# A long convolution and two MLP blocks in one kernel: the inverse transform in column tiles of TensorE, the filter's second weights in row tiles, and one merged product

## The chip, the cores and the metric

The kernel runs on one core of one Trainium2 chip. The metric is the device time of one execution in microseconds (us), given as the median of several runs; one more execution was profiled.

## The reference

```python
def _attn_ref(x, v, pos_emb, w1, w2):              # x, v: 1 x 12480 x 128
    h_mlp = np.maximum(pos_emb @ w1, 0.0) @ w2     # w1: 64 x 64, w2: 64 x 128
    h_filt = h_mlp * np.exp(-0.01 * np.arange(S))[:, None]
    u = x * v
    Uf = np.fft.rfft(u, n=2 * S, axis=1)
    Hf = np.fft.rfft(h_filt, n=2 * S, axis=0)
    y = np.fft.irfft(Uf * Hf[None, :, :], n=2 * S, axis=1)[:, :S, :]
    return x * y

def _moe_ref(x, w_in, w_out):                      # 128 -> 2048 -> 128
    r = np.maximum(x @ w_in, 0.0)
    return (r * r) @ w_out

def _moe2_ref(x, w_in, w_out):
    h = x @ w_in
    return (h / (1.0 + np.exp(-1.702 * h))) @ w_out
# output: _moe2_ref(_moe_ref(_attn_ref(...)))
```

All inputs are 32-bit floats here, except that the MLP weights arrive as 64-bit floats and are split on the chip.

## The kernel before

The long convolution is a transform of length 99 x 127 in two steps (N1 = 99, N2 = 127), with 64 folded columns (NJ). It runs in stages, all in an order written out by hand; each engine works its own queue in that order.

The filter stage (`filter_stage`, line 245) makes the hidden features of the filter. The first transform (`s1_step`, line 266) works the features and then the product of x and v: each step takes four channels, and for each channel two halves, whose 64 outputs go to partitions 0 to 63 and 64 to 127 of one PSUM tile; the two halves stand in turn in PE's order. ScalarE (ACT) copies the result to G or A (line 267). G goes through DRAM (`gd`) on SP's queue.

The frequency stage is `stage_s2`. It runs over 50 pairs p of the 99 frequencies. For each pair `spectra` multiplies the transposed features with w2b (`hk`, line 316) and the data with the coefficients (`xk`, line 318), two matmuls of 256 columns each; `back` goes back with the product P (`ob`, line 342), and every second pair `features` does four frequencies' features (`fk`, line 305, 128 columns each) for the pairs to come. A frequency's features stand in f_t as 128 rows, 64 for the cosine part and 64 for the sine part. w2b is a block matrix, 128 x 256: w2 stands in the upper left block for the cosine part, and again in the lower right one for the sine part; the rest is zero. ACT copies hk to hc (line 320), fk to fs (line 308) and ob to bs (line 346), and its queue stores bs to DRAM (`bd`) and loads `Gs`. VectorE (DVE) multiplies xk with hc in two products (line 329) and takes the difference (line 334); GpSimd (POOL) takes the sum (line 333). `load_m` (line 276) asks on SP's queue for the coefficients (m) of the pair five further on, into seven buffers; it stands behind `back(p - 2)`, which frees a buffer. `work.tick` (class `Weights`) puts one step of each running weight conversion on DVE and ACT behind each pair, and asks for raw weights on SP's queue; two chunks are left for the stage's end.

The MLP stage (`mlp`) runs over 25 tiles of about 500 positions. Each MLP has 8 units a tile, and the second one is 40 units behind the first; PE does 12 matmul records for a unit's inputs (`hin`) and outputs (`acc`, four units later), lines 488 to 490. The last step of the inverse (`inverse`, line 446) makes a tile's y in PSUM (`yps`): five segments of 98 or 99 columns, each with two accumulating fp32 matmuls over 99 rows. `front_y` calls it for tile t + 1 among the units of tile t. Two segments that are left over (`REST`) are done once, by `front_rest`. Each fp32 matmul leaves two weight loads and two matmul records in the trace; those of the MLP, in the faster 32-bit format fp32r, leave one of each.

At the seam of the two stages `load_b` reads the inverse's rows back from `bd`, DVE and POOL combine them (`combine`, line 393), and `spare` matmuls stand on PE before and behind tile 0's inverse.

Of the kernel before, what the change touches and what calls it, by code (L numbers as in the profile page):

```python
# [9 lines left out]
FP32 = mybir.dt.float32  # L10
# [4 lines left out]
ALU = mybir.AluOpType  # L15
# [8 lines left out]
N1, N2 = 99, 127  # L24
# [3 lines left out]
D = 128  # L28
F = 64
# [3 lines left out]
NP = -(-N1 // 2)  # L33
# [5 lines left out]
FK = 4  # L39
# [52 lines left out]
def conv_mlp_kernel(ctx: ExitStack, tc: tile.TileContext, xc, xt, vc, pt, w1, w2,  # L92
                    moe_w_in, moe_w_out, moe2_w_in, moe2_w_out,
                    c_s1, c_s2, c_i2, c_win, out):
    nc = tc.nc
# [5 lines left out]
    ci2 = const.tile([N1, 2, N1], FP32, name="ci2")  # L101
# [169 lines left out]
    def load_m(mp, p):  # L271
        if p >= NP:
            return
        n = min(2, N1 - 2 * p)
        m_t[p] = mp.tile([128, 2, 2, 128], FP32, tag="m", name="m", bufs=7)
        nc.sync.dma_start(out=m_t[p][:, 0:n], in_=c_s2[:, 2 * p:2 * p + n])

    def load_h(mp, g, queue=nc.scalar):
        if g >= NHL:
            return  # L280
        n = min(HL, N1 - g * HL)
        h_t[g] = mp.tile([128, HL, 2 * F], FP32, tag="Gs", name="Gs", bufs=2)
        queue.dma_start(out=h_t[g][:, 0:n], in_=gd[:, g * HL:g * HL + n])

    def stage_s2(sp, mp, A, w2b, hooks, work):


        kp = tc.tile_pool(name="kp", bufs=2, space=PSUM, reuse_waits="tile")
        obp = tc.tile_pool(name="obp", bufs=2, space=PSUM, reuse_waits="tile")
        P_t, k_t, bs_t, f_t = {}, {}, {}, {}  # L290

        def pair(p):
            return min(2, N1 - 2 * p)

        with kp as kp, obp as obp:
            def features(g):


                if g >= NFK:
                    return  # L300
                n = min(FK, N1 - g * FK)
                ps = kp.tile([128, FK, 128], FP32, tag="fk", name="fk", bufs=1)
                for i in range(n):
                    k = g * FK + i
                    nc.tensor.matmul(out=ps[:, i], lhsT=h_t[k // HL][:, k % HL, :],  # L305
                                     rhs=m_t[k // 2][:, k % 2, 0, :])
                f_t[g] = sp.tile([128, FK, 128], FP32, tag="fs", name="fs", bufs=2)
                nc.scalar.copy(out=f_t[g][:, 0:n], in_=ps[:, 0:n])

            def spectra(p):  # L310
                n, m = pair(p), m_t[p]
                xk = kp.tile([128, 2, 2, D], FP32, tag="xk", name="xk", bufs=3)
                hk = kp.tile([128, 2, 2, D], FP32, tag="hk", name="hk", bufs=2)
                for j in range(n):
                    k = 2 * p + j
                    nc.tensor.matmul(out=hk[:, j], lhsT=f_t[k // FK][:, k % FK, :], rhs=w2b)  # L316
                for j in range(n):
                    nc.tensor.matmul(out=xk[:, j], lhsT=m[:, j, 0, :], rhs=A[:, 2 * p + j])  # L318
                hc = sp.tile([128, 2, 2, D], FP32, tag="hc", name="hc", bufs=2)
                nc.scalar.copy(out=hc[:, 0:n], in_=hk[:, 0:n])  # L320
                k_t[p] = xk, hc

            def product(p):
                n = pair(p)
                xk, hc = k_t.pop(p)
                t = []
                for c in range(2):
                    t.append(sp.tile([128, 2, 2, D], FP32, tag=f"t{c}", name=f"t{c}", bufs=2))
                    nc.vector.tensor_tensor(  # L329
                        out=t[c][:, 0:n], in0=xk[:, 0:n, c].unsqueeze(2).to_broadcast([128, n, 2, D]),  # L330
                        in1=hc[:, 0:n], op=ALU.mult)
                P = sp.tile([128, 2, 2, D], FP32, tag="P", name="P", bufs=3)
                nc.gpsimd.tensor_tensor(out=P[:, 0:n, 1], in0=t[0][:, 0:n, 1], in1=t[1][:, 0:n, 0], op=ALU.add)  # L333
                nc.vector.tensor_tensor(out=P[:, 0:n, 0], in0=t[0][:, 0:n, 0], in1=t[1][:, 0:n, 1],
                                        op=ALU.subtract)
                P_t[p] = P

            def back(p):
                n, m, P = pair(p), m_t.pop(p), P_t.pop(p)
                ob = obp.tile([128, 2, 2, D], FP32, tag="ob", name="ob")  # L340
                for j in range(n):
                    nc.tensor.matmul(out=ob[:, j], lhsT=m[:, j, 1, :], rhs=P[:, j])  # L342
                g, o = divmod(2 * p, HK)
                if o == 0:
                    bs_t[g] = sp.tile([128, HK, 2, D], FP32, tag="bs", name="bs", bufs=2)
                nc.scalar.copy(out=bs_t[g][:, o:o + n], in_=ob[:, 0:n])
                if o + n == HK or p == NP - 1:
                    nc.scalar.dma_start(
                        out=bd[:, :, HK * g:HK * g + o + n].rearrange("h j k c d -> (h j) k c d"),
                        in_=bs_t.pop(g)[:, 0:o + n])  # L350

            features(0)
            for p in range(NP + 2):
                if p < NP:
                    spectra(p)
                if p % 2 == 0:
                    features(p // 2 + 1)
                if 0 <= p - 2:
                    back(p - 2)
                load_m(mp, p + 5)  # L360
                if p % 4 == 1:
                    load_h(mp, p // 4 + 2)
                if 0 <= p - 1 < NP:
                    product(p - 1)
                work.tick(p)
                for f in hooks.get(p, ()):
                    f()
            work.finish()
# [4 lines left out]
    def tile_parts(segs):  # L373

        at = 0
        for j, s, r, n in segs:
            yield j, s, r, n, at
            at += n
# [34 lines left out]
    def mlp(lp, cp):  # L413
# [26 lines left out]
        def inverse(ps, segs):  # L440


            for j, s, r, w, o in tile_parts(segs):
                b = b_t[j // JG][1][:, j % JG, 0 if s > 0 else 1]
                for c in range(2):
                    nc.tensor.matmul(out=ps[:, o:o + w], lhsT=b[:, c, :], rhs=ci2[:, c, r:r + w],  # L446
                                     start=(c == 0), stop=(c == 1))

        def front_y(t):

# [123 lines left out]
        for n in range(len(seq) + LAG):  # L574
# [3 lines left out]
            if n < len(seq):  # L578
                l, t, j = seq[n]
# [24 lines left out]
    with tc.manual_schedule():  # L604
# [13 lines left out]
        def advance():  # L618
            if steps[0] in folds:
                inputs.fold()  # L620
            inputs.load()
            steps[0] += 1

        with tc.tile_pool(name="h", bufs=1) as hp:
            h = hp.tile([N1, F, 2 * NJ], FP32, name="h")
            inputs = Inputs(up)
# [10 lines left out]
        with tc.tile_pool(name="A", bufs=1, reuse_waits="tile") as ap_, ExitStack() as mps:  # L637
            A = ap_.tile([128, N1, 2, D], FP32, name="A")
            for d in range(0, D, 4):
                s1_step(bank, inputs.u[d // XC], d % XC, A[:, :, :, d:d + 4])  # L640
                if d // 4 in (0, 3, 6, 9):
                    q = 25 * (d // 12)
                    q = slice(q, min(q + 25, N1))
                    nc.sync.dma_start(out=gd[:, q], in_=G[:, q].rearrange("p k c f -> p k (c f)"))
                if d // 4 < 22:
                    advance()
                if d // 4 == 22:
                    assert inputs.done == NXC
                    vps.close()
                    mp = mps.enter_context(tc.tile_pool(name="mh", bufs=1, reuse_waits="tile"))  # L650
                    w2b = mp.tile([128, 2 * D], FP32, name="w2b")
                    nc.sync.dma_start(out=w2b, in_=w2)
                if 22 <= d // 4 < 27:
                    load_m(mp, d // 4 - 22)
                if d // 4 in (23, 25):
                    load_h(mp, (d // 4 - 23) // 2, nc.sync)
            sgs.close()
            ups.close()
            w0 = ctx.enter_context(tc.tile_pool(name="w0", bufs=1, side="right", reuse_waits="tile"))
            split_weights(w0, 0)  # L660
            cp = ctx.enter_context(tc.tile_pool(name="cvt", bufs=1, side="right", reuse_waits="tile"))
            lp = ctx.enter_context(tc.tile_pool(name="lp", bufs=2, side="right", reuse_waits="tile"))
            nc.sync.dma_start(out=ci2, in_=c_i2)
            work = Weights([0, 4, 1, 5, 2, 6], 3, 7, 5, cp, [(44, 3), (46, 7)])
            hooks = {44: [lambda: load_x(lp, 0)]}
            with tc.tile_pool(name="s2", bufs=1, side="right", reuse_waits="tile") as sp:
                stage_s2(sp, mp, A, w2b, hooks, work)
# [92 lines left out]
```

## Time and profile before

| | |
|---|---|
| median of 3 runs | 1419.97 us (1417.61 to 1421.13) |
| profiled execution | 1419.01 us, of it 1417.2 us span |
| TensorE (PE) busy | 1399.3 us, 99% |
| VectorE (DVE) busy | 1114.3 us, 79% |
| ScalarE (ACT) busy | 940.4 us, 66% |
| frequency stage | about 90 to 242 us |
| MLP stage | from about 253 us |

Times in the rows are microseconds from the start of the span unless they are marked ns. PE is TensorE's matmuls, PEld its weight loads, which overlap with them. A matmul's recorded duration holds its way through the array, so records that follow each other overlap; what one costs is read from start to start, or from the chain. In the chain, each piece is the time that it alone added.

### The profile page before, as it was taken

How to read it: one execution, taken by the hardware profiler on the slowest of the kernel's cores; microseconds unless marked ns; L12 is line 12 of the kernel's file. 1: busy time of each engine (PE TensorE's matmuls, PEld its weight loads, DVE VectorE, ACT ScalarE, POOL GpSimd, SP SyncE). 2: the span in 40 equal slices, each digit the busy share in tenths (PEclk: the TensorE clock that was granted, in tenths of full speed). 3: DMA queues.
4: the chain of work that ended last, by engine and by line, in shares of the span. 5: the costliest groups of instructions: out<-in, count | busy, mean ns of one | idle time of the engine just before them, and what ended most of it. 6: DMA issues, size and time to landing. Idle time of an engine off the chain costs nothing.

```text
span 1417.2 us, 17764 instructions
## 1 busy us (share of the span) xinstructions
PE 1399.3 (99%) x7018; PEld 1175.7 (83%) x7018; DVE 1114.3 (79%) x1233; ACT 940.4 (66%) x1066; POOL 221.2 (16%) x209
## 2 busy tenths in 40 slices
PE   7999999999999999999999999999999999999998
PEld 7888888788788888888888888888888888888887
DVE  7558988699887777777778777777778787777887
ACT  1654544577667767776767767777777767777776
POOL 3012222425620111111100211012101120000000
PEclk9999999899999999999999999999999999999999
DMA  9977765312200001000010000010000100000000
GB/s 248 302 247 241 242 229 195 102 60 79 68 20 8 26 20 38 25 9 20 27 38 8 27 20 26 8 38 19 27 27 8 38 19 8 8 8 1 15 15 15
DMA packets 46400, 91.34 MB, mean 64 GB/s; under 512 B 4183, under 2 KB 30604, under 8 KB 45804
## 3 DMA queue, kind: packets, MB, share of 16 engines
q1 hardware_dynamic: 36750, 64.71, 15.2%
q10 hardware_dynamic: 9566, 25.49, 4.7%
q8 instruction: 55, 0.90, 0.3%
q14 instruction: 29, 0.24, 0.1%
HBM read 64.33 MB, written 25.85 MB: 64 GB/s over the span
## 4 chain that ended last, share of the span: by engine, by line
PE 92%; DVE 4%; issue 1%; DMA 1%; ACT 1%; POOL 0%; SPq 0%; DVEq 0%; POOLq 0%; ACTq 0%
PE hin L489 12%; PE hin L490 12%; PE hin L488 12%; PE acc L489 12%; PE acc L488 12%; PE acc L490 12%; PE s L266 5%; PE yps L446 4%; PE hk L316 3%; PE xk L318 3%; PE ob L342 3%; PE fk L305 2%; DVE gl L526 1%; DVE r L250 1%; DMA uv<-bd 1%
## 5 line engine op out<-in xcount | busy, mean ns | idle before, releaser
L526 DVE TENSOR_TENSOR gl<-g,gh 128x1004 fp32r<-128x1004 f32 (+4 forms) x400 | 491.7, 1229 | 34.9 <-ACT gh L522 34.5
L506 ACT ACTIVATE g<-hin 128x1004 f32<-128x1004 f32 (+4 forms) x200 | 201.2, 1006 | 238.4 <-PE hin L490 237.9
L488 PE MATMUL acc<-gh,w 128*128 128x502 f32 (+4 forms) x800 | 313.6, 392 | 0.3 <-DVE lo L435 0.3
L488 PE MATMUL hin<-hi,w 128*128 128x502 f32 (+4 forms) x800 | 312.8, 391 | 0.0
L489 PE MATMUL acc<-gl,w 128*128 128x502 f32 (+4 forms) x800 | 311.8, 390 | 0.8 <-DVE gl L526 0.8
L489 PE MATMUL hin<-lo,w 128*128 128x502 f32 (+4 forms) x800 | 312.5, 391 | 0.0
L490 PE MATMUL hin<-hi,w 128*128 128x502 f32 (+4 forms) x800 | 311.9, 390 | 0.0
L490 PE MATMUL acc<-gh,w 128*128 128x502 f32 (+4 forms) x800 | 311.7, 390 | 0.0
L517 DVE TENSOR_TENSOR g<-hin,g 128x1004 f32<-128x1004 f32 (+4 forms) x200 | 238.7, 1193 | 50.6 <-ACT g L509 50.5
L393 POOL TENSOR_TENSOR b<-uv 99x256 f32<-99x256 f32 x127 | 158.1, 1274 | 698.4 <-DMA uv<-bd 501.0
L515 DVE CAST gh<-g 128x1004 fp32r<-128x1004 f32 (+4 forms) x200 | 142.4, 712 | 149.7 <-ACT g L507 149.6
L509 ACT ACTIVATE g<-hin 128x1004 f32<-128x1004 f32 (+4 forms) x200 | 200.1, 1001 | 75.2 <-PE hin L490 67.2
L507 ACT ACTIVATE g<-g 128x1004 f32<-128x1004 f32 (+4 forms) x200 | 208.0, 1040 | 6.4
L522 ACT CAST gh<-g 128x1004 fp32r<-128x1004 f32 (+4 forms) x200 | 202.8, 1014 | 0.4 <-DVE g L517 0.4
L488 PEld LDWEIGHTS hin<-hi,w 128*128 128x128 f32 x800 | 151.4, 189 | 33.8 <-ACT g L506 2.5
L489 PEld LDWEIGHTS acc<-gl,w 128*128 128x128 f32 x800 | 151.1, 189 | 32.0 <-DVE gl L526 2.1
L490 PEld LDWEIGHTS hin<-hi,w 128*128 128x128 f32 x800 | 151.4, 189 | 30.7
L488 PEld LDWEIGHTS acc<-gh,w 128*128 128x128 f32 x800 | 151.2, 189 | 30.8 <-DVE lo L435 0.7
L489 PEld LDWEIGHTS hin<-lo,w 128*128 128x128 f32 x800 | 151.3, 189 | 30.6 <-issue 0.5
L490 PEld LDWEIGHTS acc<-gh,w 128*128 128x128 f32 x800 | 150.8, 189 | 30.4
L329 DVE TENSOR_TENSOR t<-xk,hc 128x512 f32<-128x512 f32 (+1 forms) x100 | 63.8, 679 | 23.7 <-PE xk L318 19.5
L333 POOL TENSOR_TENSOR P<-t,t 128x256 f32<-128x256 f32 (+1 forms) x50 | 43.8, 876 | 176.8 <-DVE t L329 94.5
(56 smaller groups left out, 1032.1 us busy)
## 6 DMA issues: line engine op xcount, KB each, us to landing
uv<-bd SPq DMA_DIRECT2D x64, 198.0 KB
m<-in_c_s_dram SPq DMA_DIRECT2D x49, 256.0 KB
bd<-bs ACTq DMA_DIRECT2D x24, 512.0 KB
x<-in_xc_dram SPq DMA_DIRECT2D x16, 384.0 KB
v<-in_vc_dram SPq DMA_DIRECT2D x16, 384.0 KB
Gs<-gd ACTq DMA_DIRECT2D x10, 512.0 KB
gd<-G SPq DMA_DIRECT2D x3, 1600.0 KB
raw<-in_moe_w_in_dram SPq DMA_DIRECT2D x8, 512.0 KB
```

Of the source, the lines that this page charges most:

```text
L266: nc.tensor.matmul(out=ps[j, e], lhsT=src[:, d + e, j], rhs=cs1[:, half])
L393: engine.tensor_tensor(out=b[:, :, s, c], in0=uv[:, 0, :, c], in1=uv[:, 1, :, 1 - c], op=ALU.add if s != c else ALU.subtract)
L488: nc.tensor.matmul(out=out, lhsT=a, rhs=hl[0], start=first, stop=False)
L489: nc.tensor.matmul(out=out, lhsT=a, rhs=hl[1], start=False, stop=False)
L490: nc.tensor.matmul(out=out, lhsT=b, rhs=hl[0], start=False, stop=last)
L506: nc.scalar.activation(out=g, in_=ps, func=ACTF.Relu)
L507: nc.scalar.activation(out=g, in_=g, func=ACTF.Square)
L509: nc.scalar.activation(out=g, in_=ps, func=ACTF.Sigmoid, scale=1.702)
L515: nc.vector.tensor_copy(out=gh, in_=g)
L517: nc.vector.tensor_tensor(out=g, in0=ps, in1=g, op=ALU.mult)
L522: nc.scalar.copy(out=gh, in_=g)
L526: nc.vector.tensor_tensor(out=gl, in0=g, in1=gh.bitcast(FP32), op=ALU.subtract)
```

## The change

The change has three parts.

In `inverse`, each matmul of 128 weight columns becomes two of 64 weight columns, for output partitions 0 to 63 and 64 to 127, with the same moving columns.

In the frequency stage, w2b becomes 128 x 128: w2 twice, one above the other. The matmuls for hk leave `spectra` for a new function `filters`, which works four frequencies at once, every second pair, ahead of `spectra`. For each frequency it issues two matmuls, one on the 64 rows of the cosine part and one on the 64 rows of the sine part, into two banks of PSUM. ACT copies the four frequencies' result to hc in one instruction, which also brings the two parts of a frequency next to each other. hk has one buffer of two banks instead of two buffers of one bank.

In `product`, the two products become one of 1024 elements, with both operands broadcast, into one tile t. P has two buffers instead of three.

```diff
-                hk = kp.tile([128, 2, 2, D], FP32, tag="hk", name="hk", bufs=2)
-                for j in range(n):
-                    k = 2 * p + j
-                    nc.tensor.matmul(out=hk[:, j], lhsT=f_t[k // FK][:, k % FK, :], rhs=w2b)
...
-                hc = sp.tile([128, 2, 2, D], FP32, tag="hc", name="hc", bufs=2)
-                nc.scalar.copy(out=hc[:, 0:n], in_=hk[:, 0:n])
-                k_t[p] = xk, hc
+                k_t[p] = xk
...
+            def filters(g):
+                n = min(FK, N1 - g * FK)
+                hk = kp.tile([128, 2, FK, D], FP32, tag="hk", name="hk", bufs=1)
+                for i in range(n):
+                    for c in range(2):
+                        f = slice(c * F, (c + 1) * F)
+                        nc.tensor.matmul(out=hk[:, c, i], lhsT=f_t[g][f, i, :], rhs=w2b[f])
+                h_c[g] = sp.tile([128, FK, 2, D], FP32, tag="hc", name="hc", bufs=2)
+                nc.scalar.copy(out=h_c[g][:, 0:n], in_=hk[:, :, 0:n].rearrange("p c k d -> p k c d"))
...
             def product(p):
                 n = pair(p)
-                xk, hc = k_t.pop(p)
-                t = []
-                for c in range(2):
-                    t.append(sp.tile([128, 2, 2, D], FP32, tag=f"t{c}", name=f"t{c}", bufs=2))
-                    nc.vector.tensor_tensor(
-                        out=t[c][:, 0:n], in0=xk[:, 0:n, c].unsqueeze(2).to_broadcast([128, n, 2, D]),
-                        in1=hc[:, 0:n], op=ALU.mult)
-                P = sp.tile([128, 2, 2, D], FP32, tag="P", name="P", bufs=3)
...
+                xk, o = k_t.pop(p), 2 * p % FK
+                hc = h_c[2 * p // FK][:, o:o + n]
+                t = sp.tile([128, 2, 2, 2, D], FP32, tag="t", name="t", bufs=2)
+                full = [128, n, 2, 2, D]
+                nc.vector.tensor_tensor(out=t[:, 0:n], in0=xk[:, 0:n].unsqueeze(3).to_broadcast(full),
+                                        in1=hc.unsqueeze(2).to_broadcast(full), op=ALU.mult)
+                P = sp.tile([128, 2, 2, D], FP32, tag="P", name="P", bufs=2)
...
             for p in range(NP + 2):
+                if p < NP and p % 2 == 0:
+                    filters(p // 2)
                 if p < NP:
                     spectra(p)
...
                 for c in range(2):
-                    nc.tensor.matmul(out=ps[:, o:o + w], lhsT=b[:, c, :], rhs=ci2[:, c, r:r + w],
-                                     start=(c == 0), stop=(c == 1))
+                    for d in (slice(0, D // 2), slice(D // 2, D)):
+                        nc.tensor.matmul(out=ps[d, o:o + w], lhsT=b[:, c, d], rhs=ci2[:, c, r:r + w],
+                                         start=(c == 0), stop=(c == 1))
...
-                    w2b = mp.tile([128, 2 * D], FP32, name="w2b")
+                    w2b = mp.tile([128, D], FP32, name="w2b")
...
+    laid['w2'] = np.concatenate([inputs['w2']] * 2)
```

## Rows read from the trace of the kernel before

**Rows 1.** The page's busy times by engine and the chain that ended last.
```profile
PE 1399.3 (99%) x7018; PEld 1175.7 (83%) x7018; DVE 1114.3 (79%) x1233; ACT 940.4 (66%) x1066; POOL 221.2 (16%) x209
...
PE 92%; DVE 4%; issue 1%; DMA 1%; ACT 1%; POOL 0%; SPq 0%; DVEq 0%; POOLq 0%; ACTq 0%
```

**Rows 2.** Windows of the two stages: stretch, length, then each engine's busy us.
```profile
92.36:238.80 146.44, 145.28 (x764) 130.30 (x765) 126.63 (x192) 71.79 (x124) 41.76 (x48) 1.00 0.68 229
...
600.00:1000.00 400.00, 400.00 (x1838) 333.15 (x1837) 310.44 (x306) 286.71 (x307) 50.02 (x53) 1.00 0.07 23
```

**Rows 3.** Chain in order of time, two pairs: start us, us, what, records.
```profile
102.19 0.86 PE ob L342 x4
103.05 0.86 PE hk L316 x4
...
104.78 0.89 PE fk L305 x8
```

**Rows 4.** Timeline of PE around one inverse (merged records), then that inverse's chain piece.
```profile
409.29 0.39 PE L490 MATMUL hin<-hi,w 128*128 128x502 f32 x1
409.51 2.37 PE L446 MATMUL yps<-ci,b 99*128 99x98 f32 x20
...
411.97 0.39 PE L489 MATMUL acc<-gl,w 128*128 128x492 f32 x1
...
409.68 2.21 PE yps L446 x20
```

**Rows 5.** First transform: window of line 266, its loads (ns), a timeline pair, lines.
```profile
60.00:70.00 10.00, 10.00 (x122) 8.55 (x120) 1.00 1.03 339
...
L266 PEld LDWEIGHTS s<-cs,u x120: 137/137/137, 60.0 to 69.9; 99*64 99x64 f32 x120
...
23.74 0.14 PEld L266 LDWEIGHTS s<-cs,h 99*64 99x64 f32 x2 [0.35 <-DVE h L256]
...
L305 PEld LDWEIGHTS fk<-m,Gs 128*128 128x128 f32 x198 | 26.0, 191 | 2.9 <-DMA m<-in_c_s_dram 1.3 <-issue 0.3
```

**Rows 6.** Timeline where the first transform ends and the frequency stage begins.
```profile
89.29 0.82 ACT L267 COPY A<-s 128x792 f32<-128x792 f32 x1 [0.69 <-PE s L266]
...
90.27 0.33 PE L266 MATMUL s<-cs,u 99*64 99x198 f32 x1
...
90.53 0.19 PEld L305 LDWEIGHTS fk<-m,Gs 128*128 128x128 f32 x1 [0.29 <-issue]
```

**Rows 7.** Chain from the frequency stage's end to tile 0 of the MLP.
```profile
239.72 1.30 DVE t L329 x2
...
241.45 0.77 DVE t L329 x2
...
252.57 1.30 DVE b L393 x2
253.92 4.16 PE yps L446 x18
258.08 3.28 PE spare L564 x4
```

**Rows 8.** Groups by line, forms apart: count, busy us, mean ns, idle before.
```profile
L329 DVE TENSOR_TENSOR t<-xk,hc 128x512 f32<-128x512 f32 x98 | 63.0, 684 | 23.7 <-PE xk L318 19.5 <-PE fk L305 2.0 <-ACT hc L320 1.7
L517 DVE TENSOR_TENSOR g<-hin,g 128x1004 f32<-128x1004 f32 x88 | 105.4, 1198 | 20.1 <-ACT g L509 20.1
L211 DVE TENSOR_TENSOR x<-x,v 99x1024 f32<-99x1024 f32 x16 | 19.6, 1223 | 18.4 <-DMA v<-in_vc_dram 12.7 <-DMA w2b<-in_w_dram 5.0 <-ACT G L267 0.8
L506 ACT ACTIVATE g<-hin 128x1004 f32<-128x1004 f32 x88 | 89.0, 1011 | 102.4 <-PE hin L490 102.2
L320 ACT COPY hc<-hk 128x512 f32<-128x512 f32 x49 | 28.7, 585 | 21.8 <-DVE P L334 13.0 <-PE hk L316 8.3 <-DVE t L329 0.5
```

**Rows 9.** The one late transfer of coefficients, in the chain and in PE's waits.
```profile
197.66 5.84 DMA m<-in_c_s_dram
...
PE fk L305 <- DMA m<-in_c_s_dram: 1.2, 1, 1.2
```

More of the change, by code (lines that the diff above doesn't have):

```diff
@@ L289, in stage_s2 @@
         obp = tc.tile_pool(name="obp", bufs=2, space=PSUM, reuse_waits="tile")
-        P_t, k_t, bs_t, f_t = {}, {}, {}, {}
+        P_t, k_t, bs_t, f_t, h_c = {}, {}, {}, {}, {}
         def pair(p):
@@ L312, in spectra @@
                 xk = kp.tile([128, 2, 2, D], FP32, tag="xk", name="xk", bufs=3)
-                hk = kp.tile([128, 2, 2, D], FP32, tag="hk", name="hk", bufs=2)
-                for j in range(n):
-                    k = 2 * p + j
-                    nc.tensor.matmul(out=hk[:, j], lhsT=f_t[k // FK][:, k % FK, :], rhs=w2b)
                 for j in range(n):
                     nc.tensor.matmul(out=xk[:, j], lhsT=m[:, j, 0, :], rhs=A[:, 2 * p + j])
-                hc = sp.tile([128, 2, 2, D], FP32, tag="hc", name="hc", bufs=2)
-                nc.scalar.copy(out=hc[:, 0:n], in_=hk[:, 0:n])
-                k_t[p] = xk, hc
+                k_t[p] = xk
             def product(p):
                 n = pair(p)
-                xk, hc = k_t.pop(p)
-                t = []
-                for c in range(2):
-                    t.append(sp.tile([128, 2, 2, D], FP32, tag=f"t{c}", name=f"t{c}", bufs=2))
-                    nc.vector.tensor_tensor(
-                        out=t[c][:, 0:n], in0=xk[:, 0:n, c].unsqueeze(2).to_broadcast([128, n, 2, D]),
-                        in1=hc[:, 0:n], op=ALU.mult)
-                P = sp.tile([128, 2, 2, D], FP32, tag="P", name="P", bufs=3)
-                nc.gpsimd.tensor_tensor(out=P[:, 0:n, 1], in0=t[0][:, 0:n, 1], in1=t[1][:, 0:n, 0], op=ALU.add)
-                nc.vector.tensor_tensor(out=P[:, 0:n, 0], in0=t[0][:, 0:n, 0], in1=t[1][:, 0:n, 1],
+                xk, o = k_t.pop(p), 2 * p % FK
[5 more added lines that the diff above has]
+                P = sp.tile([128, 2, 2, D], FP32, tag="P", name="P", bufs=2)
+                nc.gpsimd.tensor_tensor(out=P[:, 0:n, 1], in0=t[:, 0:n, 0, 1], in1=t[:, 0:n, 1, 0], op=ALU.add)
+                nc.vector.tensor_tensor(out=P[:, 0:n, 0], in0=t[:, 0:n, 0, 0], in1=t[:, 0:n, 1, 1],
                                         op=ALU.subtract)
@@ L738 @@
     laid['pt'] = _folded(inputs['pos_emb']).transpose(1, 3, 2, 0).reshape(2 * F, NJ, N1)
-    for name in ('w1', 'w2'):
-        f, e = inputs[name].shape
-        laid[name] = np.zeros((2, f, 2, e), np.float32)
-        for i in range(2):
-            laid[name][i, :, i] = inputs[name]
-        laid[name] = laid[name].reshape(2 * f, 2 * e)
+    f, e = inputs['w1'].shape
+    laid['w1'] = np.zeros((2, f, 2, e), np.float32)
+    for i in range(2):
+        laid['w1'][i, :, i] = inputs['w1']
+    laid['w1'] = laid['w1'].reshape(2 * f, 2 * e)
+    laid['w2'] = np.concatenate([inputs['w2']] * 2)
     given = [(n, np.ascontiguousarray(laid[n])) for n in _INS]
```

## The prediction

> **What bounds the kernel now.** I read the page's head first: TensorE (PE) is busy 99% of the span, VectorE (DVE) 79%, and the chain that ended last is PE for 92% [rows 1]. A saving in this kernel is thus PE time, wherever PE has no wait. Then I looked at the two stages that the change touches, by their windows: in the frequency stage, from 92 to 239 us, PE is busy for 145.3 of 146.4 us, DVE for 126.6, at full clock; in the body of the MLP PE is busy without a gap [rows 2]. So in both stages a microsecond off PE's order is a microsecond off the end, up to what DVE (87% of the first stage) and the transfers allow. Third, the chain piece by piece gives each kind of matmul its price: two frequencies' filter (hk) 0.86 us for 4 records, the same for the way back (ob), and 0.89 us for 8 records of fk [rows 3]. An fp32 matmul leaves two records, so a record of 256 columns takes 0.216 us and one of 128 columns 0.111 us; a moving column of one record costs about 0.00084 us. The inverse's 20 records of 98 or 99 columns take 2.21 us [rows 4], 0.110 each. By their columns they would need 0.083. They cost as much as the 128-column records of fk, and what both share is a 128-column weight load: the inverse is bound by its loads, not by its columns.
>
> **Inverse in column tiles.** The 20 records of a tile become 40, each with 64 weight columns, in turn for PSUM partitions 0 to 63 and 64 to 127. The first transform already works so (its two halves also write partitions 0 to 63 and 64 to 127 in turn): 120 loads of 64 columns in 10 us of busy PE [rows 5], so a pair takes 0.167 us, which is the time of the 198 columns of one of them. Both halves stream at once, and two loads lie within 0.14 us where one alone takes 0.137 [rows 5]. A 64-column load lasts 137 ns against 191 [rows 5], so I estimate 0.111 - 0.054 = 0.057 us for it in a row, less than a slot of columns. The slot is then 0.083 us. As the two records of a matmul follow each other, the first and the last stand alone: 21 slots, 1.74 us.
>
> The seams come on top. The only change from column tiles to the whole array in this trace is at 90.3 us: the last record of the first transform starts at 90.27 and its columns last 0.165; the copy that frees the next bank ended at 89.29 + 0.82 = 90.11; yet the load for fk starts at 90.53, put down to "issue" [rows 6]. That is 0.09 us after the columns, and the load (0.111), elsewhere hidden, stands in the open: 0.20 us a seam. The Trainium skill ("TensorEngine Tiling (Array Packing)", Key Properties) says that a change of the tiling mode drains the engine; by that rule the gap at 90.3 us is the rule's drain, and it comes twice for each stretch of tiles. The way in has no row (PE was idle before the first transform); I take the same drain and a 64-column load, 0.15, between bounds of nothing and 0.4.
>
> Now: from the start of the last record before an inverse (409.29) to the second behind it (411.97) are 2.68 us, of which two ordinary records are 0.45; the inverse costs 2.23 [rows 4]. After: 1.74 + 0.15 + 0.20 = 2.09. That saves 0.14 for each of tiles 1 to 24, 3.4 us. The two segments of the rest are 8 records now (about 0.89) and 9 slots with two seams after (1.10): +0.2. Tile 0 runs at half clock (its spare records take 0.82 us, 3.28 for 4) and takes 4.16 us for 18 records [rows 7]; 21 slots of 0.167 are 3.5, but the first records wait for the combined rows on DVE [rows 7], which don't move: I take -0.6, between 0 and -0.9. The sum for the inverse is -3.8 us.
>
> **The filter's second weights in row tiles.** For four frequencies PE now works 8 records of 256 columns against a half-empty block matrix, 2 x 0.86 = 1.73 us [rows 3]. After: 16 records of 128 columns, each on 64 rows, in turn for the upper and the lower half of the array, into two banks. No row shows row tiles. Bounds: like the column tiles, two at once, 9 slots of 0.111 = 1.00 us; or one after another, 1.78. I take the first, since the nearest row is the other tiling of the same array [rows 5]. The Trainium skill ("TensorE: Matmul & The Clock Gate", Part 3) lets loads and matmuls overlap where the row group differs; that speaks for the same end. Two seams with 128-column loads add 0.41, together 1.41: 0.32 saved in each of 24 groups, and 0.1 in the last with three frequencies: -7.8 us.
>
> **The copies and the product.** ScalarE (ACT) copies 1024 elements once per four frequencies (about 1.01 us, as for its reads of 1004 from PSUM) instead of 2 x 0.585; DVE makes one product of 1024 (1.22 us, between 1.20 for 1004 from PSUM and 1.22 for 1024 from SBUF) instead of 2 x 0.684 [rows 8]. Both lie under PE: 0.14 us of DVE for each of 50 pairs, some 7 us off its 126.6. That is what keeps DVE below PE when the stage shrinks to some 139 us: without it DVE would be at 91%, with it 86%. On the path they count at the stage's end alone, where the chain goes through DVE's products of 1.30 and 0.77 us [rows 7]: -0.2. Three buffers of P become two: a product then waits until the way back two pairs earlier is read, which PE starts right behind this pair's spectrum; the product itself lasts longer than that (1.22 against 0.86). Where fk stands between them, DVE waits up to 0.5 us, inside its slack. On ACT's queue the one copy waits for four frequencies in place of two; behind it stand the copies of fk and ob, both later on PE. SP's queue and POOL keep their instructions and order.
>
> **What is late next.** The coefficients (m) for the coming pairs are asked for when a way back frees a buffer, and PE needs them 4.6 us later: one transfer of 5.84 us made PE wait 1.2 [rows 9]. Each step now has 0.32 us less in that stretch, so this wait grows by 0.3 and others that nearly wait now may appear, 25 at most with 0.3 each: I take +1.0, between 0 and 7.5.
>
> **Sum** against the profiled run (1419.01 us, 1.0 below the median): -3.8 - 7.8 - 0.2 + 1.0 = -10.8. For the median of 1419.97 that is 1409.2 us. With a drain between 0.05 and 0.13 (four of them in a tile and a group together: 4 us either way) and the transfers' bounds, the forecast's own range is 1404 to 1416.
>
> **Rivals.**
> *The seams cost nothing* (the 0.26 us at 90.27 belong to the new PSUM pool, not to the tiling). Then the inverse goes from 2.23 to 1.82 (-9.8 for 24 tiles), tile 0 saves 0.6, a filter group goes from 1.73 to 1.00 (-18 in all), DVE's end gives 0.2, and the coefficients come late more often (+3): -25.6, 1394 us. For it: one row alone carries the drain. Against it: nothing else that PE waited for stands in the trace there.
>
> *Row tiles take turns.* Then a filter group is 16 x 0.111 + 0.41 = 2.19 us, 0.46 slower, 11.5 in all, and with -4.0 from the inverse and the product the time is 1427, slower. The point from which it decides is 0.083 us per record: above it the group costs more than 1.73.
>
> *PE can't issue records of half a slot.* The inverse would need a load and a matmul each 0.0415 us. The densest stretch of this trace has them each 0.083 [rows 5], where columns bind, so no floor between the two is excluded. The inverse breaks even at 0.047 (40 x 0.047 + 0.35 = 2.23); at 0.083 it takes 3.7, +35 us for 24 tiles, while a filter group (16 x 0.083 + 0.41) stays where it is: 1455. For it: nothing ran denser. Against it: PE has the time of the records before to take in the next ones. The Trainium skill ("TensorE: Matmul & The Clock Gate", section on 56 ns) gives about 62 ns per matmul where the engine's own program decodes them; as an estimate, 40 x 0.062 + 0.35 = 2.84, +14.6 for the tiles, +0.5 for the rest, -7.8 for the filter and +0.8 for the other two terms: 1428 us.
>
> *Seams cost twice as much* (0.4 on each side, the upper bound of the way in): a tile goes from 2.23 to 2.54 us, a filter group from 1.73 to 1.80; +7.4, +0.7 for the rest and +1.8, less 0.4 for tile 0 and the product: 1429.
>
> *The change doesn't tile at all* in effect, with halves one after the other in both places: then the second and third rivals together, over 1440; the first transform's records speak against it.
>
> **How the numbers follow.** Chances: forecast 0.52, seams free 0.15, row tiles in turn 0.10, an issue floor 0.12, dear seams 0.08, no tiling 0.03. A difference under 0.3% (4.3 us) can hardly be told from none. Faster: nearly all of the forecast and the free seams, 0.65; same: the forecast's dear end and mild forms of the floor, 0.11; slower 0.24. The range reaches to the free seams below and to the 1427 to 1429 of three rivals above; it leaves out the hard floor, the untiled case and a little below, under 2 in 10.
>
> **What would show it.** In the changed trace: 40 records of yps in a window of about 1.75 us, pairs a few ns apart each 0.083, and a gap of 0.1 to 0.2 before the load on both sides; 16 records of hk in about 1.0 us, in pairs; a product near 1.22 us; the frequency stage some 7 us shorter. Single hk records 0.11 apart, or yps records over 0.047 apart, make the prediction wrong.

## The result

The changed kernel takes 1406.0 us, the kernel before 1419.0 in the same runs: a ratio of 0.991, 95% interval 0.9897 to 0.9924, 12.8 us less (10.8 to 14.6). Forecast were 10.8 less. Run again beside the experiments below, the ratio was 0.9918 (0.9898 to 0.9939). The profiled execution of the changed kernel has a span of 1405.7 us.

Much of what one kernel's executions differ by is the clock that TensorE was granted: the six of the run with fk behind the way back, below, go from 1398.96 us at a mean granted clock of 0.998 to 1407.71 at 0.991. As PE is busy for 98% of the span, a time multiplied by its execution's mean granted clock is an estimate of the time at the full clock; for 23 executions of the kernel before it brings the standard deviation from 2.3 to 1.0 us. Where medians leave a question open, this estimate stands beside them. By it the changed kernel, run again, is 11.8 us shorter (means of 1398.2 and 1410.0).

First the chain of the changed kernel in order of time (start us, us, what, records), two pairs of the frequency stage:

```profile
105.11 1.09 PE hk L318 x16
106.20 1.06 PE xk L326 x4
107.26 0.89 PE fk L305 x8
108.15 0.87 PE ob L347 x4
109.02 0.86 PE xk L326 x4
109.88 0.86 PE ob L347 x4
```

The filter of four frequencies costs 1.09 us and, in the xk behind it, 0.20 more than an ordinary xk (1.06 against 0.86): 1.29 in place of the 1.73 of before [rows 3].

PE's timeline and chain around one inverse, for the same tile as [rows 4] (the last two lines are pieces of the chain):

```profile
401.46 0.39 PE L498 MATMUL hin<-hi,w 128*128 128x502 f32 x1
401.78 1.92 PE L454 MATMUL yps<-ci,b 99*64 99x98 f32 x40
...
403.95 0.39 PE L497 MATMUL acc<-gl,w 128*128 128x492 f32 x1
...
401.85 1.84 PE yps L454 x40
403.69 0.42 PE acc L496
```

From the last record before it (401.46) to the second behind it (403.95) are 2.49 us; less two ordinary records (0.45) the inverse costs 2.04, against 2.23 [rows 4]. The chain shows where: 1.84 for 40 records, and the first acc 0.42 in place of 0.22.

The seams themselves: the last record and the first load at the way into hk, the same at the way out, and the way into an inverse:

```profile
104.73 0.38 PE L347 MATMUL ob<-P,m 128*128 128x256 f32 x1
...
105.04 0.97 PEld L318 LDWEIGHTS hk<-w2b,fs 64*128 64x128 f32 x16 [0.33 <-issue]
...
105.93 0.27 PE L318 MATMUL hk<-w2b,fs 64*128 64x128 f32 x1
...
106.13 0.51 PEld L326 LDWEIGHTS xk<-A,m 128*128 128x128 f32 x3
...
401.78 0.20 PEld L454 LDWEIGHTS yps<-ci,b 99*64 99x64 f32 x4 [0.36 <-issue]
```

Before hk the load waits for nothing that the profile shows ("issue"), as it did at the one seam of before [rows 6]. Read record by record, with 0.00084 us for a column, a load behind a seam starts 0.093 us after the columns of the last record end: 105.93 and 128 columns (0.107) give 106.04 here, and the load starts at 106.13. It is 0.092 to 0.093 at both ends of the row tiles and 0.091 to 0.094 on the way out of the column tiles; the way into those comes behind a record of the MLP, whose load starts 0.31 to 0.32 us after it where such records stand 0.23 apart, some 0.09.

Last, PE's waits (us in total, times, longest), without those of the first stages:

```profile
PE acc L497 <- DVE gl L534: 3.5, 5, 2.3
...
PE fk L305 <- DMA m<-in_c_s_dram: 2.3, 3, 0.9
PE fk L305 <- DMA Gs<-gd: 1.2, 1, 1.2
```

Three late transfers of coefficients in place of one [rows 9]; a wait for Gs at the stage's beginning that before did not have; and more waiting for DVE in the MLP, where before it was 0.8 us. The second trace of the changed kernel, run again, has the first two too, but not the third:

```profile
PE fk L305 <- DMA m<-in_c_s_dram: 2.7, 2, 1.8
PE fk L305 <- DMA Gs<-gd: 2.3, 1, 2.3
PE acc L497 <- DVE gl L534: 0.9, 3, 0.5
```

From fk's first record to the last xk the stage takes 141.3 us where it took 150.4, and from the first yps to the end the MLP takes 1158.1 where it took 1164.1, but 4 to 5 us of that are chance. In the profiled execution of before PE waited for the combined rows of one inverse (at 365.7 us), and right behind these waits the granted clock was half (1.2 GHz) for 6.8 us:

```profile
PE yps L446 <- POOL b L393: 1.7, 3, 1.2
PE acc L489 <- DVE gl L526: 0.8, 2, 0.5
...
369.50:376.30 6.80, 6.69 (x19) 5.65 (x20) 3.61 (x5) 0.00 (x0) 5.05 (x7) 0.50 0.37 112
```

Of the four runs below with the old inverse three have neither (their MLP stages take 1159.4 to 1159.8 us); the one with m moved down has the waits and not the fall (1161.6). Against this, the frequency stage begins 3.2 us later (93.69 against 90.53): 1.3 of it is a longer gap behind the first transform, and 1.9 came before, where traces with the same first stages also differ (the transform's last record starts at 89.2 to 93.4 us in all the traces here).

### The profile page after: what moved, and what is told of

Read it like the earlier page. It is cut to its first block, busy times and chain, and to the rows that moved or that the text cites. A ratio compares the mean times of both kernels' runs of the same rounds, so it can differ in the third digit from the quotient of the medians.

```text
span 1405.7 us, 19120 instructions
## 1 busy us (share of the span) xinstructions
PE 1383.6 (98%) x7724; PEld 1153.5 (82%) x7724; DVE 1114.3 (79%) x1183; ACT 937.3 (67%) x1041; POOL 226.8 (16%) x209
## 4 chain that ended last, share of the span: by engine, by line
PE 87%; DVE 6%; DMA 4%; issue 1%; ACT 1%; SPq 0%; DVEq 0%; ACTq 0%
PE acc L496 12%; PE hin L497 12%; PE hin L496 12%; PE hin L498 12%; PE acc L497 12%; PE acc L498 12%; PE xk L326 3%; PE yps L454 3%; PE ob L347 3%; PE s L266 2%; DVE gl L534 2%; PE hk L318 2%; PE fk L305 2%; DMA m<-in_c_s_dram 1%; DMA x<-in_xc_dram 1%
## 5 line engine op out<-in xcount | busy, mean ns | idle before, releaser
L523 DVE CAST gh<-g 128x1004 fp32r<-128x1004 f32 (+4 forms) x200 | 145.8, 729 | 143.0 <-ACT g L515 142.9
L338 POOL TENSOR_TENSOR P<-t 128x256 f32<-128x256 f32 (+1 forms) x50 | 48.4, 968 | 165.8 <-DVE t L335 121.4
L335 DVE TENSOR_TENSOR t<-xk,hc 128x1024 f32<-128x1024 f32 (+1 forms) x50 | 60.3, 1205 | 14.6 <-ACT hc L320 10.1
```

Source lines behind the costliest of these rows:

```text
L335: nc.vector.tensor_tensor(out=t[:, 0:n], in0=xk[:, 0:n].unsqueeze(3).to_broadcast(full), in1=hc.unsqueeze(2).to_broadcast(full), op=ALU.mult)
L523: nc.vector.tensor_copy(out=gh, in_=g)
```

## The experiments

Each was timed in several rounds beside the kernel before. Where two of them are compared, their medians or their traces are, and the text says which.

**The inverse alone.** The kernel before with this edit:

```diff
-                    nc.tensor.matmul(out=ps[:, o:o + w], lhsT=b[:, c, :], rhs=ci2[:, c, r:r + w], ...)
+                    for d in (slice(0, D // 2), slice(D // 2, D)):
+                        nc.tensor.matmul(out=ps[d, o:o + w], lhsT=b[:, c, d], rhs=ci2[:, c, r:r + w], ...)
```

> The kernel before with the inverse alone in column tiles; the frequency stage is as before. Theory (the parts add up, each on PE's order): a tile's inverse costs 2.05 us in place of 2.23, so 24 x 0.19 = 4.5, tile 0 gives 0.5 and the rest takes 0.1: 4.9 us less than before, 1414.1, ratio 0.9965. Rival (PE's savings in the MLP are eaten by waits on DVE): under 2 us less, over 1417. Rival (it also takes away the waits for combined rows that the kernel before had at tile 5, some 2 us): 7 us less, 1412.

Measured: 1412.8 us, ratio 0.9969 (0.9957 to 0.998), 4.4 us less (2.8 to 6.1). The first theory's 4.9 lies in the interval; the rivals' under 2 and 7 do not. Its inverses cost what those of the changed kernel do, and its waits on PE show what this execution gave back:

```profile
PE acc L490 <- DVE gl L527: 3.0, 3, 2.1
```

**The filter and the product alone.** The changed kernel with the old inverse.

> The changed kernel with the inverse as before: row tiles, groups of four and the merged product alone. Theory (parts add up): a filter group costs 1.29 us in place of 1.73, so 24 x 0.44 + 0.2 = 10.8 less, and later coefficients give back 1.5 to 2: 9 us less than before, 1410, ratio 0.9937. Rival (the gain of the stage is mostly DVE's, freed by the merged product): the same time, but then the run with the merged product alone shows it too. Rival (transfers bound the stage): 5 us less or fewer, 1414 and above.

Measured: 1411.5 us, ratio 0.9965 (0.9952 to 0.9978), 5.0 us less (3.1 to 6.8). The theory's 9 is refuted in size: the stage itself got shorter as expected (142.5 us from the first fk to the last xk), but it began late, and that was not in my sum. The time alone fits the second rival's 5 us as well (transfers); in the trace a transfer did cost it, but mostly the one that the stage begins with, not those within it (1.1 us):

```profile
PE fk L305 <- DMA Gs<-gd: 2.5, 1, 2.5
PE fk L305 <- DMA m<-in_c_s_dram: 1.1, 1, 1.1
```

What made it late, and what the lateness cost, is further down (where the m buffers lie). The two parts alone give 4.4 + 5.0 = 9.4 us; together they gave 11.6 to 12.8, inside what the intervals leave.

**The product alone.** The kernel before with one product of 1024 elements and two buffers of P.

> The kernel before with the merged product alone (and two buffers of P). Theory (DVE lies under PE): a product of 1.2 us in place of two of 0.68, DVE some 7 us less busy, and the time stays, -0.2 us: 1418.8, ratio 1.000. Rival (DVE's lateness holds PE in the frequency stage): 3 us less or more, ratio 0.998 or below. Rival (two buffers of P make DVE wait for the way back and PE for DVE): 2 us more or worse.

Measured: ratio 1.0009 (0.9998 to 1.002): no gain, and if anything 1 us of loss. DVE's group in this run (count, busy us, mean ns, idle before) shows what the missing third buffer costs:

```profile
L332 DVE TENSOR_TENSOR P<-t 128x256 f32<-128x256 f32 (+1 forms) x50 | 21.1, 423 | 9.4 <-PE ob L340 5.2
```

and that of before:

```profile
L334 DVE TENSOR_TENSOR P<-t,t 128x256 f32<-128x256 f32 (+1 forms) x50 | 21.1, 422 | 1.7
```

DVE sat idle for 9.4 us before its differences, where before it was 1.7 us, mostly for the way back that frees P. The wait of which I wrote is there, and PE shows no wait for it: the frequency stage takes 151.5 us against 150.4, and 151.6 in the run with the inverse alone, which leaves that stage as it was. DVE's gain is hidden too, and it is smaller than I wrote: its products are busy for 60.6 us in place of 63.8.

**Groups without row tiles.** Filters of four frequencies ahead of the pairs, but each one a matmul of 256 columns over the whole array; w2b and the inverse are the old ones, and ACT copies each pair (the matmul's part of the edit):

```diff
-                    for c in range(2):
-                        f = slice(c * F, (c + 1) * F)
-                        nc.tensor.matmul(out=hk[:, c, i], lhsT=f_t[g][f, i, :], rhs=w2b[f])
+                    nc.tensor.matmul(out=hk[:, i], lhsT=f_t[g][:, i, :], rhs=w2b)
```

> The kernel before with the filter in groups of four frequencies ahead of the pairs and the merged product, but with the block matrix of 256 columns on the whole array as before, no row tiles (ACT copies each pair by itself). Theory (row tiles carry the filter's gain): a group still costs 1.73 us of PE, the time stays within 1 us: 1418 to 1420, ratio 0.9995 to 1.0005. Rival (the grouping itself, by looser waits of the copies, gives the gain): 4 us less or more, ratio 0.997 or below.

Measured: ratio 0.9997 (0.9981 to 1.0013). Grouping and product give nothing; the filter's gain is that of the row tiles. The one copy for four frequencies, which also differs, was not run by itself; the chain puts the gain on PE's hk.

**Twice the seams.** The changed kernel with each group cut in two, the second half behind the even pair's xk (the calls; `filters` does its half of the matmuls, and copies after the second):

```diff
...
                 if p < NP and p % 2 == 0:
-                    filters(p // 2)
+                    filters(p // 2, 0)
                 if p < NP:
                     spectra(p)
+                if p < NP and p % 2 == 0:
+                    filters(p // 2, 1)
```

> The changed kernel with each filter group cut in two halves of two frequencies, the second behind the even pair's spectrum: the same records, 25 more stretches of row tiles. Theory (a change of the tiling costs PE the drain of 0.093 us and the load of 0.107 us that is otherwise hidden, at each end): 0.40 us for each further stretch, 25 x 0.40 = 10 us more than the changed kernel, 1416. Rival (the gap at a seam is the new operands' wait, not the tiling's): under 3 us more, below 1409. Rival (the drain is longer after short stretches): 15 us more.

Measured: 1415.8 us, beside 1407.2 for the changed kernel on the same chip (ratio 0.9984, 0.9969 to 1.0, against 0.9918): 8.6 us more. Its chain:

```profile
109.84 0.65 PE hk L320 x8
110.49 1.06 PE xk L330 x4
...
105.51 0.65 PE hk L320 x8
106.16 1.09 PE fk L305 x8
```

Each stretch of 8 records costs 0.65 + 0.20, so two cost 1.70 where one of 16 costs 1.29: 0.41 for a stretch's two seams, 10 us for 25 of them. The rival without a price of the seam would have given under 1409, the one with a longer drain 15 us more.

**The order of the rows.** The changed kernel with the loops turned round:

```diff
-                for i in range(n):
-                    for c in range(2):
+                for c in range(2):
+                    for i in range(n):
```

> The changed kernel with the loops of the filter's matmuls turned round: all four frequencies for the upper rows first, then all four for the lower rows. Theory A (PE starts records strictly in the order of the program, so two lie side by side only where neighbours differ in their rows): one pair in eight at most, 16 x 0.111 + 0.40 = 2.2 us for a group in place of 1.29, 22 us more, 1428. Theory B (each half of the array takes its own next record, past those that wait for the other half): 8 pairs as now, 1.29 us, the time stays at 1406. In between, where it looks only a few records ahead.

Measured: 1420.6 us, ratio 1.001 (0.9995 to 1.0025), 13.4 more than the changed kernel beside it. Neither theory: a group costs 1.64 + 0.20 = 1.84 us, between 1.29 and 2.2. Its chain piece, then two windows of one group (stretch, length, busy us and records of PE and of PEld):

```profile
130.44 1.64 PE hk L318 x16
132.08 1.06 PE xk L326 x4
...
130.36:130.88 0.52, 0.51 (x4) 0.51 (x5) 1.00 0.73 280
130.88:131.32 0.44, 0.44 (x9) 0.44 (x9) 1.00 0.03 9
```

and the same of the changed kernel:

```profile
105.24:105.58 0.34, 0.34 (x8) 0.34 (x8) 1.00 0.59 223
```

In the turned order four records run alone; then the first record for the lower rows, the ninth in the program, starts 6 ns after the fifth. The trace does not name the rows; I know it by its 373 ns in place of 272, which the first records of both halves have in the changed kernel too. They hold its load, so its columns run beside those of the sixth. Five records' columns thus run alone, then three pairs (the dense window, whose counts take in records under way), and the last five are alone again: 13 slots of 0.111 us in place of 8, in 23 of the 24 full groups (the first group's clock falls in its midst). The last group, with six records for each half, has its record of 373 ns beside the third: four ahead again. PE did look past the upper rows' records, but only four records ahead.

**fk behind the way back.** The changed kernel with `features` below `back(p - 2)`:

```diff
-                if p % 2 == 0:
-                    features(p // 2 + 1)
                 if 0 <= p - 2:
                     back(p - 2)
+                if p % 2 == 0:
+                    features(p // 2 + 1)
```

> The changed kernel with the features for the coming pairs (fk) behind the way back (ob), not ahead of it: PE needs the coefficients 0.87 us later, and some of the buffers are asked for 0.89 us earlier. Theory (the late coefficients cost the stage its waits): the three waits of 0.9 to 1.1 us that the changed kernel's trace shows go, 2 to 3 us less than it: 1403 to 1404. Rival (the transfers are bound by their rate, the wait moves elsewhere): the same 1406.

Measured: 1403.8 us, 3.4 less than the changed kernel beside it; the ratios (0.9897, 0.9873 to 0.9922, against 0.9918, 0.9898 to 0.9939) overlap. The estimate at the full clock is 1395.9 against 1398.2 (standard deviations 0.9 and 1.1 us, 6 and 5 executions): 2.4 less, as the theory said. The trace has the sign:

```profile
PE fk L305 <- DMA m<-in_c_s_dram: 0.4, 1, 0.4
```

0.4 us in place of 2.3 and 2.7 in the two traces of the changed kernel, and 1.1 in that of the filter alone.

**Where the m buffers lie.** All six traces above of kernels with row tiles (two of them of the changed kernel) began the frequency stage late: 1.6 to 2.8 us lie between the last record of the first transform and the first of fk, against 0.26 in each without. SP's queue of the changed kernel, then of the one before, and DVE's last folds of the inputs (x times v, then line 213) in the same order:

```profile
83.34 6.49 SPq L276 DMA_DIRECT2D m<-in_c_s_dram  x2
89.86 0.43 SPq L283 DMA_DIRECT2D Gs<-gd  x1
...
86.15 0.69 DVE L213 TENSOR_TENSOR u<-x 99x512 f32<-99x512 f32 x1
...
88.78 0.69 DVE L213 TENSOR_TENSOR u<-x 99x512 f32<-99x512 f32 x1
```

```profile
81.46 3.70 SPq L276 DMA_DIRECT2D m<-in_c_s_dram  x2
85.20 0.43 SPq L283 DMA_DIRECT2D Gs<-gd  x1
...
84.12 0.69 DVE L213 TENSOR_TENSOR u<-x 99x512 f32<-99x512 f32 x1
...
86.96 0.69 DVE L213 TENSOR_TENSOR u<-x 99x512 f32<-99x512 f32 x1
```

Before, the second m goes out right after the fold of chunk 14 (84.12 + 0.69 = 84.81, issue at 84.83); in the changed kernel right after that of chunk 15 (88.78 + 0.69 = 89.47, issue at 89.49), and Gs behind it. The allocations say why: w2b shrank from 1024 to 512 bytes a partition, so the m buffers behind it moved down by 512. The second m's had begun exactly where chunk 14's x began, at 133600; at 133088 it also lies on the last 512 bytes of chunk 15's x. Two runs test this. First, the kernel before with m moved down alone:

```diff
-                    w2b = mp.tile([128, 2 * D], FP32, name="w2b")
+                    load_m(mp, 0)
+                    w2b = mp.tile([128, 2 * D], FP32, name="w2b")
...
-                if 22 <= d // 4 < 27:
+                if 23 <= d // 4 < 27:
```

> The kernel before with the coefficients' buffers (m) at addresses 1024 B lower: the first of them is allocated ahead of w2b, and nothing else changes (w2b keeps its size and is loaded right behind the first m). The second m's buffer, which lay exactly on the place of chunk 14's x, then also lies on that of chunk 15's x, the last one. Theory (the narrower w2b of the change moved m down by 512 B with this effect): its load, and Gs behind it on SP's queue, go out after the last fold of the inputs, not the one before, some 2.9 us later; the frequency stage begins 2 to 3 us later, 1421. Rival (the later begin of the stage in the changed kernels is chance of the first stages' transfers): the time of before, 1418 to 1419, and the second m goes out as before.

Measured: the second m goes out at 87.62 us, behind chunk 15's fold (86.91 + 0.69 = 87.60), and Gs at 88.00:

```profile
86.91 0.69 DVE L213 TENSOR_TENSOR u<-x 99x512 f32<-99x512 f32 x1
...
87.62 0.33 SPq L276 DMA_DIRECT2D m<-in_c_s_dram  x1
88.00 0.42 SPq L283 DMA_DIRECT2D Gs<-gd  x1
```

The first fk stands 1.58 us behind the first transform in place of 0.26. The mechanism is as said, its size smaller than I wrote, for Gs now lands little later than PE would have come; the ratio of 1.001 (0.9998 to 1.0022) is that of 1.4 us or of none; the estimate at the full clock is 1.7 us more (12 and 17 executions). One thing more differs than I wrote: w2b now lies on chunk 14's place and is loaded at 84.90 in place of 79.78; the second m comes 2.7 us behind it.

Second, the changed kernel with m where it lay:

```diff
-    cs1 = const.tile([N1, 2, 2 * N1], FP32, name="cs1")
...
+        cs1 = ups.enter_context(tc.tile_pool(name="cs1", bufs=1, side="right")).tile([N1, 2, 2 * N1], ...)
...
-                    w2b = mp.tile([128, D], FP32, name="w2b")
+                    w2b = mp.tile([128, 2 * D], FP32, name="w2b")[:, 0:D]
```

> The changed kernel with w2b's tile as wide as before (half of it is used), so that the m buffers lie on the inputs' places as before; cs1 moves to a pool that is given up with the transforms, to make room. Theory: the second m and Gs go out behind chunk 14's fold again, the frequency stage begins 2 to 3 us earlier than in the changed kernel, 1403 to 1404. Rival (chance): the changed kernel's 1406 to 1407.

Measured: 1401.6 us, ratio 0.9873 (0.9856 to 0.989). PE's waits:

```profile
PE acc L496 <- DVE gl L533: 2.7, 4, 1.8
...
PE fk L304 <- DMA m<-in_c_s_dram: 0.8, 2, 0.6
```

No wait for Gs is left, and the first fk stands 0.25 us behind the first transform. It gained more than that wait (1.2 and 2.3 us in the two traces of the changed kernel): late coefficients are rarer too. Why they are, I did not test; the requests for m and raw weights that pile up behind the late Gs are one candidate.

The clock is another part of the gain. In the four traces in which PE stood for 2.3 to 2.5 us before the first fk (the changed kernel run again, the filter alone, the turned order, fk behind the way back) the granted clock falls to half (1.2 GHz) for 6.8 us, between 0.4 us before the first fk and 2.3 us behind it. With m moved down alone, after a wait of 1.3 us, it falls for 3.4 us; in the two other traces with row tiles, after 1.2 us, and in the six without a late begin it stays full there. That the wait makes it fall is read from these traces and was not tested by itself. The chain of the changed kernel run again, then one stretch in it and in the trace shown first:

```profile
94.47 2.06 PE fk L305 x8
...
97.19 2.08 PE hk L318 x16
99.27 2.00 PE xk L326 x4
```

```profile
94.50:101.00 6.50, 5.83 (x28) 5.02 (x29) 0.00 (x0) 1.60 (x2) 0.00 (x0) 0.50 0.96 326
```

```profile
94.50:101.00 6.50, 5.82 (x53) 4.88 (x53) 3.11 (x4) 2.57 (x4) 1.15 (x2) 1.00 0.97 335
```

From the first fk to the fifth pair's xk that trace takes 15.2 us, where the one shown first takes 12.4: 2.8 us more, beyond the wait. In the trace of the filter alone the two, 2.5 and 2.9, more than cover the 4.0 us by which it fell short.

**Both.** The kernel with m where it lay (e10 in the words below) and fk behind the way back as well (e7):

> The kernel of e10 with fk behind ob as in e7. Theory: both gains add, 2.6 and 2.5 to 3.4 us less than the changed kernel, 1400 to 1402. Rival (an earlier begin of the stage only makes it wait for coefficients): 1403 to 1404, no better than e7.

Measured: 1400.7 us, ratio 0.9868 (0.9853 to 0.9883), the fastest here, 18.7 us less than before. The time is the theory's, though m in its place had given more than forecast. Whether the gains add is not shown: against the kernel before, the single edits take 3.0 and 6.4 us more off than the changed kernel by the ratios, and both 7.1; by the estimate at the full clock 2.4 and 3.6, and both 5.3. With m in its place, fk behind ob gives 0.8 us more by the medians, and the two can't be told apart. PE still waits for coefficients in both (0.8 and 0.6 us).

## Why the prediction was right, point by point

| term | forecast | measured | from |
|---|---|---|---|
| a filter group | 1.73 to 1.41 us, -7.8 in all | 1.29, -10.8 | chain pieces, 24 x 0.44 + 0.2 |
| an inverse | 2.23 to 2.09, -3.4 for 24 | 2.04, -4.5 | timelines, 24 x 0.19 |
| rest and tile 0 | +0.2 and -0.6 | +0.1 and -0.3 (-0.5, and 0.25 more for the spare records behind its seam) | traces of both |
| a seam's drain | 0.09 | 0.093 | records, both ways in and out |
| seams together | 0.35 and 0.41 | 0.41 a stretch | twice the seams |
| product and copies | -0.2 | none to be seen | product alone |
| late coefficients | +1.0 | +1.1 and +1.5 (2.3 and 2.7 against 1.2) | PE's waits, two traces |
| stage's late begin | not seen | +1.3 and 2.3, and 2.8 for the clock behind the second | records, SP's queue, two traces |
| waits for DVE in the MLP | not seen | +2.7 and +0.1 (3.5 and 0.9 against 0.8) | PE's waits, two traces |

*What bounds the kernel.* Right: what left PE's order left the end. The changed kernel's frequency stage has DVE busy for 122.5 of 141.3 us, 87%, and 86% were forecast. The 7 us that the merged product was to take off DVE were 3 to 4, though: the two products take 1.30 us in the chain [rows 7], less than 2 x 0.684, as records that follow each other overlap; one takes 1.22.

*Column tiles.* Right, down to the slot: 40 records in 1.84 us with the way in. *Row tiles* had no row, and the nearest one, the other tiling of the array, was the right one to take: pairs 6 ns apart, each 0.111.

*The odd slot* is the term that was mis-sized. I counted 9 slots for 16 records and 21 for 40, since I took PE to keep the order of the program, in which two records for the same half follow each other. It runs 8 pairs and 20: the record for the other half is only two places further on, and PE starts it beside the first. That is 0.11 us a group and 0.08 an inverse, 4.7 us in all, and it covers two losses that my sum did not have, so the total came out nearer than its parts.

*The seam.* The one row at 90.3 us was worth its place: drain and open load came back at every seam. The Trainium skill's drain at a change of the mode ("TensorEngine Tiling (Array Packing)", Key Properties) agrees with the trace, at 0.093 us. That ruled out "the seams cost nothing" (whose 1.82 for an inverse is 0.08 above the 1.74 of the same slots, without a reason given) and "twice as much". Tile 0's own seam stood at nothing in the sum.

*What is late next.* The size came out, and that is luck, for the mechanism is not shown: two or three transfers were late in the traces of the changed kernel, 2.3 and 2.7 us. I had put it down to the shorter steps; the run with m in its place has the same short steps and waits for 0.8, less than the 1.2 of before. What grew the wait came with the late begin.

*What the sum did not have.* I read the change of w2b's size as nothing. It moved the buffers behind it by 512 bytes, across the end of another tile: a wait that no line of the diff names. Behind the longer of these waits the clock was half, which my sum did not have either. And in the MLP, PE came to matmuls whose operands DVE makes: one wait of 1.8 to 2.3 us, some 130 us into the stage, stands in six of the eight traces with the new inverse and in none of the five with the old one. It does not come with the new inverse alone: the changed kernel run again and the last run have 0.8 us at most there. The stage takes 1157.0 us in the mean of the eight, from 1154.5 to 1158.7, where three with the old inverse take 1159.4 to 1159.8; of the 4.9 us that the inverses were to give, some 2 are missing in that mean. Their place is read from waits and was not tested by itself.

*The rival of the issue floor* is refuted: 40 records with their loads run 0.042 us apart. The 62 ns or so per matmul of the Trainium skill ("TensorE: Matmul & The Clock Gate", section on 56 ns) do not bind here; whether PE took the records in ahead of time or decodes them faster, these runs do not tell apart.

## What to carry to other kernels

A matmul with half the rows or half the columns pays in tiles if its stretch is long enough: here a stretch's two seams cost 0.41 us, and records must alternate between the halves closely, since PE looked only four records ahead. Put as much as PSUM holds into one stretch. When a tile changes its size, look at what lies behind it in memory and whose place that was: a buffer that reaches 512 bytes into a tile that is given up later waits for it, and everything behind its request on the queue waits too. Count the clock with such a wait: behind 2.3 to 2.5 us in which PE stood at the stage's begin, half the clock for 6.8 us took 2.8 us more.

## What the runs showed of the hardware that I had not expected

TensorE does not start records in the order of the program where tiles differ. With the rows in turn, pairs start 6 ns apart from the first record on; with eight records for the upper rows ahead of eight for the lower, the ninth starts beside the fifth, so it looked four records ahead, no further. The Trainium skill ("TensorE: Matmul & The Clock Gate", Part 3) has matmuls keep their order in start and end; the run with the turned order differs (13 slots of 0.111 us, where strict order would need 15 or 16), and the measurement decides.

The drain at a seam was the same, 0.091 to 0.094 us, into and out of row tiles and out of column tiles, and after a stretch of 8 records as after one of 40; into column tiles it was some 0.09.
